# An early place for one expert's second weights, zero matmuls in one unit, and copies moved between engines, in a three-stage fp32 kernel

## The chip, the cores and the metric

The kernel runs on one core of a Trainium2 chip. The metric is the device time of one execution in microseconds (us). The kernel before was timed three times: 311.83, 313.52 and 314.58 us, median 313.52 us. One more execution was taken with the hardware profiler; its rows are what the prediction rests on.

## The reference

Three stages follow each other, all in fp32.

```python
# 1. attention-like recurrence: 4 batches x 8 heads, 768 tokens, head size 40
for t in range(S):
    m_new = maximum(f[t] + m, i[t])
    C = exp(f[t] + m - m_new) * C + exp(i[t] - m_new) * outer(v[t], k[t])
    n = exp(f[t] + m - m_new) * n + exp(i[t] - m_new) * k[t]
    y[t] = sigmoid(o[t]) * (C @ q[t]) / maximum(abs(n @ q[t]), 1)
# 2. soft mixture of 8 experts with 4 slots each, on the 3072 tokens x 320 features
logits = x @ phi
d = softmax(logits, over tokens)
slot_input = d.T @ x                      # 32 slots x 320
slot_out[e] = relu(slot_input[e] @ w1[e]) @ w2[e]     # 320 -> 1024 -> 320
x = softmax(logits, over slots) @ slot_out
# 3. feed-forward: 320 -> 1024 -> 320
h = x @ w_in
u = h * softmax(h)
out = ((u - mean(u)) / sqrt(var(u) + 1e-6) * g_ln) @ w_out
```

## The kernel before

The 3072 tokens are cut into 24 units of 128 (4 batches times 6 pieces of the sequence); `U[u]` holds what belongs to unit u. The program is one straight list of instructions for each engine, written out by hand: nothing is reordered later, so each engine works through its own list and waits where a buffer or an input is not ready.

**Stage 1, the units.** The loop at line 642 runs over the units. For unit i the strings in `ORDER` (line 32, taken in turn by i modulo 4) name the steps in the order in which they are issued, and `ops` (line 571) maps the names: `scA`, `scB` are the score products of unit i+1 (line 250), `R` the decay matrix of unit i+2 (lines 218, 219), `exp` its exponential on ScalarE (line 223), `wA`, `wB` the products of both on VectorE (line 254), `o0` to `o3` and `u0` to `u3` the outputs and state updates (lines 268, 271, 278), `sig0` to `sig2` the sigmoid of unit i+1 on ScalarE (lines 229, 231), `xT` the transpose of the finished unit i-2 (line 335). The inputs of a unit come in as `qk` (three buffers) and `kvo` (four buffers), issued two units ahead at the start of unit i (lines 138 to 144); tiles of the first expert weights, `w1s` (line 436), and raw 64-bit words of `w_in` and `w_out` (line 440) come in between. All transfers are issued by the SP queue, in order. They signal on eight semaphores in turn, so a transfer is issued only when the eighth before it has landed. Small transfers `gr` (line 196, 4 KB each) spread rows of the gates over partitions.

**Stage 2.** After the units come the softmax over tokens, `slot_input`, and the expert products: `w1_mm` (line 756) for both halves of the hidden layer, transposes (`hidden_T`), copies into `h2` (`hidden_ev`), then `w2_mm` (line 804). `w2_mm(0, ...)` uses the even experts 0, 2, 4, 6, four matmuls to a row block f; `w2_mm(1, ...)` the odd experts 1, 3, 5, 7. The eight tiles `w2s` (1280 KB each) stand where stage 1 had its buffers: the pool `p1` is closed at line 788 and the pool `tl` takes its space. Each load waits until the stage-1 tiles under it have been used for the last time. They are issued in the order 0, 2, 4, 6, 1, 3, 5, 7, and the last, expert 7, lies over `x_t`, which holds hidden values, and over `raw_t`, which holds the last tile of `w1`.

`wh` and `wl` (lines 815, 816) are the rounded upper part and the rest of `w_out`; `pe_cT` and `st_cT` (lines 428, 433) transpose the combine weights and copy them to `cT`; `sw` is `slot_out` times `w_in`.

**Stage 3.** For each unit: h (line 872), maximum, exponential, u, transposes (line 916), and three matmuls for each of the eight row blocks (lines 931 to 933), in the order of the strings `FIN_START` and `FIN`. It begins with the first h at about 190.6 us and is the same code before and after.

The places that the change touches in the code of before:

```python
    cT = cpool.tile([128, NU, 128], F32R, tag="cT", name="cT")         # line 77
    for e in order:                                                     # line 800
        SP.dma_start(out=w2s[e], in_=w2[e].rearrange("(c p) d -> p c d", p=128))
    w2_mm(0, range(1))                                                  # line 811
    hidden_ev(1, hidden_T(1))
    w2_mm(0, range(1, FC))
    w2_mm(1, range(FC))
    V.tensor_tensor(out=wl, in0=wo, in1=wh.bitcast(F32), op=ALU.subtract)
```

Of the kernel before, what the change touches and what calls it, by code (L numbers as in the profile page):

```python
# [7 lines left out]
F32 = mybir.dt.float32  # L8
F32R = mybir.dt.float32r
# [4 lines left out]
ALU = mybir.AluOpType  # L14
# [4 lines left out]
T = 128  # L19
NC = S // T  # L20
NU = NB * NC
NR = NH // 2
DV = D + 1
DM = NH * D
DF = 1024
NE, NS = 8, 32
FC = DF // 128
# [4 lines left out]
ORDER = (  # L32
# [4 lines left out]
)  # L37
HALVED = (0,)
# [6 lines left out]
def tile_kernel(  # L45
# [15 lines left out]
    V, A, G, PE, SP = nc.vector, nc.scalar, nc.gpsimd, nc.tensor, nc.sync  # L61

    cpool = ctx.enter_context(tc.tile_pool(name="cpool", bufs=1))
# [10 lines left out]
    hsel = cst[:, 432:440]  # L74
    bsel = cst[:, 440:444]
    phi_sb = cpool.tile([128, 3, NS], F32, tag="phi", name="phi_sb")
    cT = cpool.tile([128, NU, 128], F32R, tag="cT", name="cT")
    ones = cpool.tile([128, 128], F32, tag="ones", name="ones")
    one1 = cpool.tile([1, 1], F32, tag="one1", name="one1")
    acc = cpool.tile([128, DM + 1], F32, tag="acc", name="acc")  # L80
    sbd = cpool.tile([128, 20, 8], F32, tag="sbd", name="sbd")
    win = cpool.tile([128, 5, 512], F32, tag="win", name="win")
    wo = cpool.tile([128, FC, DM], F32, tag="wo", name="wo")
# [196 lines left out]
    def st_cd(u):  # L280
        c, b = divmod(u, NB)
        if c == 0 or c == NC - 1:
            return
        n = 64 + D
        U[u]["cd"] = cd_t
        EE("cd").tensor_tensor(out=U[u]["cd"][0:n], in0=C_t[b][0:n], in1=NAT[c][0:n, 64 + b * NR:64 + (b + 1) * NR].unsqueeze(2).to_broadcast([n, NR, 2 * DV]), op=ALU.mult)
# [141 lines left out]
            PE.transpose(ps[:, 128 * j:128 * j + 128], cs_t[g][:, j].rearrange("p q k s -> p (q k s)").bitcast(F32), ident)  # L428
        GR[g]["cTp"] = ps

    def st_cT(g):
        out, in_ = cT[:, 4 * g:4 * g + 4, :].rearrange("p j t -> p (j t)"), GR[g]["cTp"]
        A.copy(out=out, in_=in_)

    def load_w1(n):
        SP.dma_start(out=w1s[:, n, :], in_=w1p[n])

    def load_raw(n):
        raw = raw_t
# [41 lines left out]

    load_gates(0, T)
    V.memset(acc, 0.0)
    warm = ps_o.tile([128, 512], F32, tag="po", name="warm")

    def warm_up(n):
        for _ in range(n):
            PE.matmul(warm[:, 0:DM], acc[:, 0:128], acc[:, 0:DM], start=True, stop=True)

# [81 lines left out]
    def ops(i):  # L571
        c, b = divmod(i, NB)
        prv, nx1, nx2 = i >= 1, i + 1 < NU, i + 2 < NU
        T = {}
        for r in range(4):
            T[f"o{r}"] = lambda r=r: pe_out(i, r)
            T[f"u{r}"] = lambda r=r: pe_upd(i, r)
        T["cd"] = lambda: st_cd(i)
        if i >= 2:
            T["xT"] = lambda: pe_xT(i - 2)  # L580
            T["xTc"] = lambda: st_xT(i - 2)
        if prv:
            T["numa"] = lambda: st_num(i - 1, (0,))
            T["numb"] = lambda: st_num(i - 1, (1,))
            T["C"] = lambda: st_state(i - 1)
            for k in range(3):
                T[f"den{k}"] = lambda k=k: st_den(i - 1, k)
            T["sg"] = lambda: st_sg(i - 1)
            T["x"] = lambda: st_x(i - 1)
        if nx1:  # L590
            if i > 0:
                T["scA"] = lambda: pe_scores(i + 1, 0)
                T["scB"] = lambda: pe_scores(i + 1, 1)
            T["wA"] = lambda: st_w(i + 1, 0)
            T["wB"] = lambda: st_w(i + 1, 1)
            T["kw"] = lambda: st_kw(i + 1)
            for k in range(3):
                T[f"sig{k}"] = lambda k=k: st_sig(i + 1, (k,))
        else:
            T["scA"] = lambda: wo_mean(range(3))  # L600
        if nx2:
            T["R"] = lambda: pe_decay(i + 2)
            T["exp"] = lambda: st_exp(i + 2)
        dn = (i - 2) // 2 if 1 <= i < 22 else -1
        if dn >= 0:
            if i % 2 == 0:
                T["D0"] = lambda: decode(dn, 0)
            else:
                for n, k in (("D1", 1), ("D1b", 1.5), ("D2", 2), ("D3", 3), ("D4", 4)):
                    T[n] = lambda k=k: decode(dn, k)  # L610
        if i < 2:
            for k in range(1, 9):
                T[f"G{k}"] = lambda k=k: gate(128, S, k)
            for k in range(2):
                T[f"p{k}h"] = lambda k=k: gate_hi(128, S, k)
                T[f"p{k}l"] = lambda k=k: gate_lo(128, S, k)
        if i == 1:
            T["right"] = lambda: gate_right(1, range(NH))
        elif i > 1 and b and c + 2 < NC:
            js = [range(3 * b - 3, min(3 * b, NH)), range(4 * b - 8, 4 * b - 4)][i < NB]  # L620
            T["right"] = lambda: gate_right(c + 2, js)
        if i == 1 or b == 0 and 2 <= c + 1 < NC:
            T["left"] = lambda: gate_left(c + 1)
        ng = 1 if i == 2 else c + 1 if b == 0 and i else NC
        if ng < NC:
            T["gn"] = lambda: pe_gate(ng)
            T["gnc"] = lambda: gate_nat(ng)
        if i % 2 == 1 and i < 20:
            T["lraw"] = lambda: load_raw((i - 1) // 2)
        g = (i - 5) // 4  # L630
        if g >= 0:
            for k in range(3):
                T[f"tm{k}"] = lambda k=k: tok_max(g, k)
            T["lt"] = lambda: pe_logit(g)
            T["ltc"] = lambda: st_logit(g)
            T["nt"] = lambda: pe_natural(g)
            T["ntc"] = lambda: st_natural(g)
            T["sl"] = lambda: pe_slots(g)
            T["acc"] = lambda: st_acc(g)
        return T  # L640

    for i in range(NU):
        if 2 <= i < NU - 2:
            load_qk(i + 2)
            load_kvo(i + 2)
        if i == NU - 2:
            SP.dma_start(out=w1l, in_=w1p[19])
        T_ = ops(i)
        for t in ORDER[i % NB].split():
            if t in T_:  # L650
                T_[t]()
        if 3 <= i < 18:
            load_w1(i + 1)
        if i >= NU - 2:
            for f in range(FC // 2 * (i - NU + 2), FC // 2 * (i - NU + 3)):
                A.activation(out=wo[:, f, :], in_=wo[:, f, :], func=AF.Copy, scale=gl[:, f:f + 1])
# [131 lines left out]
    p1_ctx.close()  # L788
    w1_ctx.close()
    fin = ctx.enter_context(tc.tile_pool(name="fin", bufs=1, reuse_waits="tile"))  # L790

    tl_ctx = ExitStack()
    tl = tl_ctx.enter_context(tc.tile_pool(name="tl", bufs=1, side="right", reuse_waits="tile"))
    order = (0, 2, 4, 6, 1, 3, 5, 7)
    w2s = {7: tl.tile([128, FC, DM], F32, tag="w2s7", name="w2s7")}
    h2 = tl.tile([128, FC, 4, 2, 8], F32, tag="h2", name="h2")
    V.memset(h2, 0.0)
    for e in order[-2::-1]:
        w2s[e] = tl.tile([128, FC, DM], F32, tag=f"w2s{e}", name=f"w2s{e}")
    for e in order:  # L800
        SP.dma_start(out=w2s[e], in_=w2[e].rearrange("(c p) d -> p c d", p=128))
    wh = fin.tile([128, FC, DM], F32R, tag="wh", name="wh")
    wl = fin.tile([128, FC, DM], F32R, tag="wl", name="wl")
    def w2_mm(e2, fs):
        for f in fs:
            for m in range(4):
                PE.matmul(so_ps[32 * m:32 * m + 8, 0:DM], h2[:, f, m, e2, :], w2s[2 * m + e2][:, f, :], start=e2 == 0 and f == 0, stop=e2 == 1 and f == FC - 1)  # L807

    hidden_ev(0, hT0)
    V.tensor_tensor(out=wo, in0=wo, in1=wm.unsqueeze(1).to_broadcast([128, FC, DM]), op=ALU.subtract)  # L810
    w2_mm(0, range(1))
    hidden_ev(1, hidden_T(1))
    w2_mm(0, range(1, FC))
    w2_mm(1, range(FC))
    A.copy(out=wh, in_=wo)
    V.tensor_tensor(out=wl, in0=wo, in1=wh.bitcast(F32), op=ALU.subtract)
    scratch = fin.tile([128, DF], F32R, tag="u", name="scratch", bufs=3)
    one_hot = scratch[:, 0:768].rearrange("p (j k s) -> p j k s", j=4, k=3)
    eye4 = ident.rearrange("p (j s) -> p j s", j=4).unsqueeze(2).to_broadcast([128, 4, 2, NS])
# [26 lines left out]
    V.tensor_tensor(out=swl, in0=swc_ps, in1=swh.bitcast(F32), op=ALU.subtract)  # L846
    for k in range(2, 4):
        pe_cT(k)
    for k in range(2, 4):
        st_cT(k)  # L850
    sw = [fin.tile([128, 512], F32R, tag=f"swf{n}", name=f"swf{n}") for n in range(2)]
    for n in range(2):
        sw_ps = bank(("po", "pr")[n], f"sw_ps{n}")
        for j in range(2):
            for x, src in enumerate((swh, swl)):
                lhs = one_hot[:, 2 * n + j, 1 - x:3 - x].rearrange("p a s -> p (a s)")
                PE.matmul(sw_ps[:, 256 * j:256 * j + 256], lhs, src, start=x == 0, stop=x == 1)
        cp[n](sw[n], sw_ps)
    for k in range(4, NC):
        pe_cT(k)  # L860
        st_cT(k)
    tl_ctx.close()
    ps_ctx.close()

# [179 lines left out]
```

## Time and profile before

| | |
|---|---|
| median of three runs | 313.52 us (311.83 to 314.58) |
| the profiled execution, its own time | 316.18 us |
| span of the profile, first to last instruction | 314.4 us |
| TensorE (PE) busy | 296.1 us, 94% of the span |
| VectorE (DVE) busy | 244.6 us, 78% |
| ScalarE (ACT) busy | 217.1 us, 69% |
| GpSimd (POOL) busy | 72.1 us, 23% |
| transferred | 52.06 MB |
| first unit ends, last unit ends, first h of stage 3 | about 20, 153 and 190.6 us |

A busy PE is not PE at its peak: the profile counts an instruction as busy from its start to its modelled end. PEclk is the clock granted to TensorE, as a share of 2.4 GHz (1.00, or 0.50 for 1.2 GHz). PEld are the weight loads that go with the matmuls; in fp32 each matmul stands as two records. SPq is the queue that issues transfers. A note in square brackets gives the idle time of the engine just before the row and what ended it.

### The profile page before, as it was taken

The page shows a single profiled execution, that of the slowest core. Times are in us where ns is not written, and L with a number is a line of the kernel's source. Part 1 is how long each engine was busy: PE and PEld are TensorE (multiplying, and loading weights), DVE is VectorE, ACT ScalarE, POOL GpSimd, SP SyncE. Part 2 cuts the span into 40 slices and gives each one's busy share as a digit, 9 for nine tenths or more (in the row PEclk, how much of TensorE's full clock was granted, in tenths as well). Part 3 has the DMA queues.
Part 4 walks back from the last instruction along what each step waited for, and adds up shares of the span by engine and source line. Part 5 has one row for each costly group of instructions (what it writes and reads, how often), then busy time and mean ns, then how long its engine had stood idle before and what let it go on. Part 6 is the DMA issues. An engine that isn't in the chain of part 4 may idle for free.

```text
span 314.4 us, 8424 instructions
## 1 busy us (share of the span) xinstructions
PE 296.1 (94%) x3333; PEld 236.4 (75%) x3333; DVE 244.6 (78%) x526; ACT 217.1 (69%) x469; POOL 72.1 (23%) x105
## 2 busy tenths in 40 slices
PE   7985999988999999989999797999999999999995
PEld 4564787765787777767642345999999999999995
DVE  8688589876899999999658417998888787787851
ACT  5375576647667757858624527798898888988983
POOL 5412064454355465364102200000000000000000
PEclk9997599997999999999999999999999999999999
DMA  6976788888999998778998500011011011010111
GB/s 166 277 174 260 222 269 286 238 294 240 285 281 292 292 305 286 240 229 272 364 361 302 170 2 0 0 46 42 24 41 44 21 44 43 21 44 25 41 42 42
DMA packets 26086, 52.06 MB, mean 166 GB/s; under 512 B 3904, under 2 KB 15872, under 8 KB 26048
## 3 DMA queue, kind: packets, MB, share of 16 engines
q1 hardware_dynamic: 26048, 51.53, 51.4%
q8 instruction: 26, 0.43, 0.6%
q14 instruction: 12, 0.10, 0.1%
HBM read 47.03 MB, written 3.93 MB: 162 GB/s over the span
## 4 chain that ended last, share of the span: by engine, by line
PE 74%; DVE 10%; DMA 8%; ACT 3%; issue 2%; POOL 1%; SPq 1%; POOLq 0%; ACTq 0%; DVEq 0%
PE o L933 9%; PE o L931 9%; PE o L932 9%; PE uT L916 7%; PE sc L250 7%; PE po L268 5%; DMA kvo<-kvo 4%; PE h L872 3%; PE R L218 3%; PE xTp L335 3%; PE R L219 3%; DMA w2s<-w 2%; PE pr L271 2%; DVE lb L254 2%; PE so_ph L807 1%
## 5 line engine op out<-in xcount | busy, mean ns | idle before, releaser
L931 PE MATMUL o<-wh,uh 128*128 128x320 f32 x192 | 62.9, 327 | 0.0
L933 PE MATMUL o<-wh,ul 128*128 128x320 f32 x192 | 59.2, 308 | 0.0
L932 PE MATMUL o<-wl,uh 128*128 128x320 f32 x192 | 58.9, 307 | 0.0
L891 DVE SCALAR_TENSOR_TENSOR u<-h,e 128x1024 f32<-128x1024 f32 (+1 forms) x25 | 29.4, 1181 | 16.4 <-ACT e L884 16.4
L268 PE MATMUL po<-kvo,lb 128*64 128x41 f32 x768 | 38.4, 232 | 0.8 <-PE sc L250 0.8
L250 PE MATMUL sc<-qk 64*128 64x128 f32 x384 | 35.7, 308 | 2.1 <-DMA qk<-qkp 1.8
L254 DVE TENSOR_TENSOR lb<-sc,lb 128x512 f32<-128x512 f32 x48 | 31.3, 676 | 7.6 <-PE sc L250 4.8
L932 PEld LDWEIGHTS o<-wl,uh 128*128 128x128 f32 x192 | 36.2, 188 | 0.9
L931 PEld LDWEIGHTS o<-wh,uh 128*128 128x128 f32 x192 | 36.1, 188 | 0.9
L250 PEld LDWEIGHTS sc<-qk 64*128 64x128 f32 x384 | 28.8, 205 | 10.5 <-issue 3.8
L268 PEld LDWEIGHTS po<-kvo,lb 128*64 128x64 f32 x768 | 31.1, 141 | 6.7 <-issue 3.2
L933 PEld LDWEIGHTS o<-wh,ul 128*128 128x128 f32 x192 | 36.0, 187 | 0.0
L924 DVE TENSOR_TENSOR ul<-uT,uh 128x512 fp32r<-128x512 f32 x48 | 33.0, 688 | 3.3 <-ACT uh L920 3.3
L920 ACT CAST uh<-uT 128x512 fp32r<-128x512 f32 x48 | 28.1, 585 | 9.4 <-PE uT L916 8.7
L231 ACT ACTIVATE kvo<-kvo 128x320 f32<-128x320 f32 x48 | 22.6, 472 | 16.7 <-DMA kvo<-kvo 16.2
L916 PE MATMUL uT<-cst,u 128*128 128x128 f32 x192 | 28.8, 273 | 1.6 <-DVE u L891 1.6
L877 DVE TENSOR_REDUCE st<-h 128x1 f32<-128x1024 f32 x24 | 29.2, 1215 | 1.4 <-PE h L872 1.4
L884 ACT ACTIVATE e<-h,st 128x1024 f32<-128x1024 f32 (+1 forms) x25 | 26.7, 1069 | 3.5 <-DVE st L877 3.3
L903 ACT ACTIVATE e<-u,st 128x1024 f32<-128x1024 f32 x24 | 27.7, 1154 | 1.9 <-DVE st L897 1.9
L223 ACT ACTIVATE lb<-R 128x1024 f32<-128x1024 f32 x24 | 24.3, 1012 | 5.8 <-PE R L219 5.7
L218 PE MATMUL R<-gr,gl 128*128 128x512 f32 x48 | 26.3, 607 | 0.0
L916 PEld LDWEIGHTS uT<-cst,u 128*128 128x128 f32 x192 | 23.8, 141 | 2.2 <-DVE u L891 2.0
(241 smaller groups left out, 587.4 us busy)
## 6 DMA issues: line engine op xcount, KB each, us to landing
kvo<-kvo SPq DMA_DIRECT2D x24, 484.0 KB
w2s<-w SPq DMA_DIRECT2D x8, 1280.0 KB
w1s<-w1p SPq DMA_DIRECT2D x19, 512.0 KB
raw<-w SPq DMA_DIRECT2D x10, 512.0 KB
qk<-qkp SPq DMA_DIRECT2D x24, 160.0 KB
qk<-qkp SPq DMA_DIRECT2D x48, 80.0 KB
out<-ob SPq DMA_DIRECT2D x24, 160.0 KB
gt<-gates SPq DMA_DIRECT2D x1, 640.0 KB
```

Of the source, the lines that this page charges most:

```text
L218: PE.matmul(U[u]["R"][:, a], gl_t[c % 2][:, b, :], gr_t[c % 2][:, a * NR:(a + 1) * NR, :], start=True, stop=False)
L250: PE.matmul(U[u]["sc", a][:, r, :], t[p, 0, r, :], t[p, 1, r, :], start=True, stop=True)
L254: V.tensor_tensor(out=lb[:, a * NR:(a + 1) * NR, :], in0=U[u]["sc", a], in1=lb[:, a * NR:(a + 1) * NR, :], op=ALU.mult)
L268: PE.matmul(U[u]["po"][t, 2 * r + a, :], U[u]["lb"][:, a * NR + r, t], va(u, 2 * r + a), start=True, stop=True)
L877: V.tensor_reduce(out=F[i]["st"][:, 0:1], in_=F[i]["h"], axis=AX.XY, op=ALU.max, negate=True)
L891: V.scalar_tensor_tensor(out=F[i]["u"][:, c], in0=F[i]["h"].rearrange("p n f -> p (n f)")[:, c], scalar=1.0, in1=F[i]["e"][:, c], op0=ALU. ...
L916: PE.transpose(ps[:, k, :], F[i]["u"][:, (4 * n + k) * 128:(4 * n + k + 1) * 128], ident)
L920: A.copy(out=F[i]["uh"][:, 4 * n:4 * n + 4, :], in_=F[i]["uT", n])
L924: V.tensor_tensor(out=F[i]["ul"][:, c, :], in0=F[i]["uT", n], in1=F[i]["uh"][:, c, :].bitcast(F32), op=ALU.subtract)
L931: PE.matmul(o, uh, wh[:, k, :], start=k == 0, stop=False)
L932: PE.matmul(o, uh, wl[:, k, :], start=False, stop=False)
L933: PE.matmul(o, ul, wh[:, k, :], start=False, stop=k == FC - 1)
```

## The change

Five edits. (1) `w2s0`, expert 0 of the second weights, has its own tile, and is loaded at the end of unit 1; the other seven stay in the `tl` pool. (2) `cT` leaves the first pool, to make room for it, and stands in the last pool, `fin`. (3) `wl` is computed by GpSimd instead of VectorE; three instead of one row blocks of `w2_mm(0, ...)` stand ahead of the transposes of the second half. (4) Two of the six copies to `cT` go to VectorE, and one of ScalarE's comes after its copy of `sw`. (5) Six matmuls on a tile of zeros (128 x 320 each) stand in unit 2 ahead of `xT`; their result isn't used.

```diff
- "numa D1b xT tm1 scA numb D1 C scB den0 xTc tm2 D2 nt ntc sig0 den1 R o0 den2 o1 gn gnc sl sg sig1 u3 kw o3 wA wB cd o2 x exp acc u1 u2 u0 D0 sig2 right",
+ "numa D1b W xT tm1 scA numb D1 C scB den0 xTc tm2 D2 nt ntc sig0 den1 R o0 den2 o1 gn gnc sl sg sig1 u3 kw o3 wA wB cd o2 x exp acc u1 u2 u0 D0 sig2 right",
...
-    cT = cpool.tile([128, NU, 128], F32R, tag="cT", name="cT")
+    w2s0 = cpool.tile([128, FC, DM], F32, tag="w2s0", name="w2s0")
...
-    def st_cT(g):
+    def st_cT(g, eng=1):
         out, in_ = cT[:, 4 * g:4 * g + 4, :].rearrange("p j t -> p (j t)"), GR[g]["cTp"]
-        A.copy(out=out, in_=in_)
+        cp[eng](out, in_)
...
+    w2s = {0: w2s0}
+
+    def load_w2(e):
+        SP.dma_start(out=w2s[e], in_=w2[e].rearrange("(c p) d -> p c d", p=128))
...
-    warm = ps_o.tile([128, 512], F32, tag="po", name="warm")
-
-    def warm_up(n):
+    def warm_up(n, tag="po"):
+        warm = ps_o.tile([128, 512], F32, tag=tag, name=f"warm_{tag}{n}")
         for _ in range(n):
             PE.matmul(warm[:, 0:DM], acc[:, 0:128], acc[:, 0:DM], start=True, stop=True)
...
+        if i == 2:
+            T["W"] = lambda: warm_up(6, "misc")
...
+        if i == 1:
+            load_w2(0)
...
+    cT = fin.tile([128, NU, 128], F32R, tag="cT", name="cT")
...
-    w2s = {7: tl.tile([128, FC, DM], F32, tag="w2s7", name="w2s7")}
...
-    for e in order[-2::-1]:
+    for e in order[:0:-1]:
         w2s[e] = tl.tile([128, FC, DM], F32, tag=f"w2s{e}", name=f"w2s{e}")
-    for e in order:
-        SP.dma_start(out=w2s[e], in_=w2[e].rearrange("(c p) d -> p c d", p=128))
+    for e in order[1:]:
+        load_w2(e)
...
-    w2_mm(0, range(1))
+    w2_mm(0, range(3))
     hidden_ev(1, hidden_T(1))
-    w2_mm(0, range(1, FC))
+    w2_mm(0, range(3, FC))
...
-    V.tensor_tensor(out=wl, in0=wo, in1=wh.bitcast(F32), op=ALU.subtract)
+    G.tensor_tensor(out=wl, in0=wo, in1=wh.bitcast(F32), op=ALU.subtract)
...
-    for k in range(2, 4):
-        st_cT(k)
+    st_cT(2, 0)
...
         cp[n](sw[n], sw_ps)
+    st_cT(3)
     for k in range(4, NC):
         pe_cT(k)
-        st_cT(k)
+        st_cT(k, k % 2)
```

The SP queue at the end of unit 1 and in units 2 and 3, before (`raw` are the raw words, `qk_0_123` and `kvo_116` the inputs of unit 4, `qk_0_121` and `kvo_115` those of unit 5):

```order
L440 DMA raw_94<-w 128x1024
L138 DMA qk_0_123<-qkp 40x1024
L140 DMA qk_0_123<-qkp 40x512 x2
L144 DMA kvo_116<-kvo 128x968
L196 DMA gr_77<-m_130 8x128 x4
L138 DMA qk_0_121<-qkp 40x1024
L140 DMA qk_0_121<-qkp 40x512 x2
L144 DMA kvo_115<-kvo 128x968
```

The same place after:

```order
L445 DMA raw_94<-w 128x1024
L441 DMA w2s_63<-w 128x8x320
L138 DMA qk_0_123<-qkp 40x1024
L140 DMA qk_0_123<-qkp 40x512 x2
L144 DMA kvo_116<-kvo 128x968
L196 DMA gr_77<-m_130 8x128 x4
L138 DMA qk_0_121<-qkp 40x1024
L140 DMA qk_0_121<-qkp 40x512 x2
L144 DMA kvo_115<-kvo 128x968
```

The transfer of expert 0 (`w2s_63`) now stands ahead of the inputs of unit 4, and one of the four small `gr` transfers behind them is the eighth after it.

The SP queue at the end of stage 1, before (`raw` here is the last tile of `w1`; the number after `w2s` is the expert):

```order
L647 DMA raw0_94<-w1p 128x1024
L801 DMA w2s0_2422<-w2 128x8x320
L801 DMA w2s2_2421<-w2 128x8x320
L801 DMA w2s4_2420<-w2 128x8x320
L801 DMA w2s6_2419<-w2 128x8x320
L801 DMA w2s1_2418<-w2 128x8x320
L801 DMA w2s3_2417<-w2 128x8x320
L801 DMA w2s5_2416<-w2 128x8x320
L801 DMA w2s7_2413<-w2 128x8x320
```

The same place after:

```order
L653 DMA raw0_94<-w1p 128x1024
L441 DMA w2s2_2431<-w2 128x8x320
L441 DMA w2s4_2430<-w2 128x8x320
L441 DMA w2s6_2429<-w2 128x8x320
L441 DMA w2s1_2428<-w2 128x8x320
L441 DMA w2s3_2427<-w2 128x8x320
L441 DMA w2s5_2426<-w2 128x8x320
L441 DMA w2s7_2425<-w2 128x8x320
```

Seven loads are left, and each expert takes the place in memory, and with it the wait, that the one ahead of it in the list had: expert 2 that of expert 0, and so on, expert 7 that of expert 5. The place of expert 7, over `x_t` and `raw_t`, is left free.

TensorE at the start of unit 2, before (`dps` ends unit 1, `xTp` is the transpose of unit 0, `sc` the scores of unit 3):

```order
L278 MATMUL dps<-kvo_115 40x41 x4
L335 MATMUL xTp_398<-cst,x_92 128x128 x3
L250 MATMUL sc_0_402<-qk_0_125 128x128
L250 MATMUL sc_1_403<-qk_0_125 128x128
L250 MATMUL sc_0_402<-qk_0_125 128x128
```

The same place after:

```order
L278 MATMUL dps<-kvo_115 40x41 x4
L492 MATMUL warm_misc_400<-acc 128x320 x6
L335 MATMUL xTp_407<-cst,x_92 128x128 x3
L250 MATMUL sc_0_411<-qk_0_125 128x128
L250 MATMUL sc_1_412<-qk_0_125 128x128
```

The six matmuls on zeros stand between the last update of unit 1 and the transpose of unit 0.

## Rows read from the trace of the kernel before

**Rows 1.** The page's slices: granted TensorE clock, in tenths, 40 slices.

```profile
PEclk9997599997999999999999999999999999999999
```

**Rows 2.** Chain of waits, 172 to 191 us: start, us, what.

```profile
172.45 7.42 DMA w2s<-w
...
188.99 1.07 ACT cT L433 x2
190.06 0.54 ACT swf L729
```

**Rows 3.** Timeline of the weight loads, 172 to 180 us: start, us, instruction, idle before.

```profile
172.94 0.20 PEld L766 LDWEIGHTS hT<-cst,acc 128*128 128x128 f32 x2 [0.67 <-ACT acc L754]
...
177.45 0.10 PEld L807 LDWEIGHTS so_ph<-w2s,h 128*8 128x8 f32 x3 [0.17 <-issue]
179.91 0.12 PEld L807 LDWEIGHTS so_ph<-w2s,h 128*8 128x8 f32 x8 [2.36 <-DMA w2s<-w]
```

**Rows 4.** SP queue, 160 to 173 us: what it waited for (us, times, longest).

```profile
SPq L801 <- PE ph L761: 2.6, 1, 2.6
```

**Rows 5.** SP queue, timeline, 161 to 163 us: the seventh load of `w2s`.

```profile
161.80 1.69 SPq L801 DMA_DIRECT2D w2s<-w  x1
```

**Rows 6.** Windows: PE, PEld, DVE, ACT, POOL busy, then granted clock, DMA share, GB/s.

```profile
26.00:28.00 2.00, 0.00 (x0) 0.00 (x0) 1.97 (x5) 1.48 (x5) 0.73 (x1) 0.92 1.01 410
32.00:34.00 2.00, 2.00 (x19) 1.08 (x17) 0.42 (x1) 0.00 (x0) 0.00 (x0) 0.50 0.91 294
34.00:36.00 2.00, 2.00 (x34) 1.93 (x32) 0.76 (x2) 1.11 (x3) 0.00 (x0) 0.50 0.83 286
36.00:38.00 2.00, 2.00 (x19) 1.44 (x14) 1.50 (x3) 1.98 (x4) 0.00 (x0) 0.52 0.61 201
38.00:40.00 2.00, 2.00 (x35) 1.49 (x33) 1.37 (x6) 1.78 (x4) 0.94 (x1) 1.00 0.46 68
...
72.00:74.00 2.00, 1.92 (x6) 1.18 (x6) 1.25 (x4) 1.97 (x4) 0.00 (x0) 0.52 0.85 312
...
168.00:170.00 2.00, 2.00 (x21) 0.48 (x14) 1.72 (x5) 0.52 (x2) 0.00 (x0) 1.00 1.07 362
```

**Rows 7.** Timeline of PE at 28 and 41 us.

```profile
28.13 0.90 PE L335 MATMUL xTp<-cst,x 128*128 128x128 f32 x3 [3.15 <-POOL x L330]
...
40.95 0.50 PE L218 MATMUL R<-gr,gl 128*128 128x512 f32 x1
```

**Rows 8.** Timeline of the SP queue, 30 to 39 us.

```profile
30.38 0.45 SPq L440 DMA_DIRECT2D raw<-w  x1
...
32.11 0.35 SPq L144 DMA_DIRECT2D kvo<-kvo  x1
...
38.18 0.35 SPq L144 DMA_DIRECT2D kvo<-kvo  x1
```

**Rows 9.** SP queue, 36 to 40 us: what it waited for.

```profile
SPq L144 <- DMA kvo<-kvo: 1.9, 1, 1.9
```

**Rows 10.** Timeline of ACT, 38 to 41 us.

```profile
38.19 0.47 ACT L231 ACTIVATE kvo<-kvo 128x320 f32<-128x320 f32 x1 [0.21 <-DMA kvo<-kvo]
...
39.07 1.01 ACT L223 ACTIVATE lb<-R 128x1024 f32<-128x1024 f32 x1
```

**Rows 11.** Timeline of PE at 150 us: six records of 128 x 320 matmuls.

```profile
149.90 1.78 PE L478 MATMUL warm<-wo,bsc 128*128 128x320 f32 x6
```

**Rows 12.** Timelines of POOL at 39 us, of DVE from 176 us, of PE at 197 us.

```profile
39.05 1.27 POOL L463 TENSOR_TENSOR win<-win,dsc 128x512 f32<-128x512 f32 x1 [7.92 <-DVE win L459]
...
176.64 2.83 DVE L816 TENSOR_TENSOR wl<-wo,wh 128x2560 fp32r<-128x2560 f32 x1 [2.63 <-ACT wh L815]
184.43 0.49 DVE L823 COPY so_sb<-so_ph 128x320 f32<-128x320 f32 x1 [4.96 <-PE so_ph L807]
...
197.42 0.31 PE L932 MATMUL o<-wl,uh 128*128 128x320 f32 x1
```

**Rows 13.** Chain of waits, 60 to 69 us.

```profile
62.04 6.52 DMA kvo<-kvo
```

## The prediction

> **What bounds the kernel now.** I read the page's slices first, then the chain of waits, then the timeline of the stretches that the change touches, and last the SP queue, since two of the five edits move transfers. The slices [rows 1] show a TensorE that holds its full clock, 2.4 GHz, in nearly every slice; the dents are one in slices 4 and 5 (31 to 39 us, units 2 and 3) and one around 72 us. TensorE is the engine that the chain mostly runs over, so what an edit is worth is the time by which TensorE's list moves, in stage 1 and at the change to stage 3 apart.
>
> Three places matter. First, the end of stage 2: the chain sits for 7.42 us on the last load of second expert weights [rows 2]. It was issued only at 172.45 us, because the queue first waited 2.6 us for a matmul of L761 [rows 4]. Not all of it is lost: TensorE worked through what it had, and its weight loads stood idle for 2.36 us, from the group at 177.45 us until 179.91 us [rows 3]. Between groups in this loop 0.16 to 0.17 us is usual, so the lost time is 2.36 - 0.16 = 2.2 us.
>
> Second, unit 2: TensorE has nothing to do for 3.15 us, until GpSimd has written x at about 28.1 us [rows 7]. The granted clock falls during that idle time: the window from 26 to 28 us has 0.92, so the drop came 2 x 0.08 / 0.5 = 0.3 us before its end. It is 0.50, which is 1.2 GHz, until shortly before 38 us (36 to 38 us still 0.52) [rows 6]. That is some 10.2 us at half clock.
>
> Third, the transfers of units 2 and 3. The inputs `kvo` of unit 4 are issued at 32.11 us and are what ScalarE waits for at 38.19 us; the SP queue itself waits 1.9 us for the same transfer before it issues the next `kvo` at 38.18 us [rows 8 to 10]. So `kvo` of unit 4 landed at 38.1 us, and behind it on ScalarE stands the exponential of unit 5 (39.07 us, ending at 40.08), which frees the bank that TensorE's next decay matrix needs: that one starts at 40.95 us [rows 7, 10]. The slack of this path against TensorE is only 40.95 - 40.08 = 0.87 us.
>
> **The change part by part.** The sum is made against the profiled execution, 316.18 us; the median of the runs is 2.66 us lower, and I carry the difference over to it.
>
> (a) *Seven loads at the end instead of eight.* Each expert takes the place, and so the wait, of the one ahead of it in the list. Expert 7 gets that of expert 5, whose load was issued at 161.80 us [rows 5] instead of 172.45 us. The transfers stand queued from there: 362 GB/s at 168 to 170 us with a DMA share of 1.07 [rows 6], so one load of 1.31 MB takes 1.31 / 362 = 3.6 us; the load that was issued at 161.80 us in this trace was used at 177.45 us without a wait [rows 3]. The 2.2 us are gone, and I find nothing else late behind them: the experts of the even half are each in earlier than before. What comes next is TensorE's own list.
>
> (b) *Three row blocks ahead of the second transposes.* The weight loads stood idle for 0.67 us before L766 at 172.94 us, waiting for ScalarE [rows 3]. Against the 0.16 us that are usual, 0.2 to 0.5 us of it can be filled with matmuls that have to run anyway. I take 0.2, since part of the idle time is the start of a transpose on any order. (a) and (b) together: -2.4 us, bounds -1.8 (a little of the wait turns up again on the copies into `h2`) and -2.8.
>
> (c) *`wl` on GpSimd.* VectorE took 2.83 us for it [rows 12]. GpSimd takes 1.27 us for 512 columns of two inputs, so five times that, 6.35 us, for 2560. It starts when `wh` is done, 176.64 us in this trace and half a microsecond later behind (b), and ends about 183.5 us; the first matmul that needs it is L932 at 197.42 us [rows 12]. More than 10 us of cover; 0. VectorE gains nothing, since its next work, the copy at 184.43 us, waited 4.96 us for TensorE anyway [rows 12].
>
> (d) *Copies to `cT`.* On the chain, ScalarE's two copies at 188.99 us are followed by its copy of `sw` at 190.06 us [rows 2]. Taken out of the way, the copy of `sw` still needs its matmuls, which end at about the same time. Gain at most the 0.3 us of one short wait, loss at most 0.2 us if the copy on VectorE holds up its own half of `sw`; I take 0.
>
> (e) *Six zero matmuls.* They are 12 records, and six records of this shape take 1.78 us at full clock [rows 11], so 12 take 3.6 us at most. The gap is 3.15 us [rows 7], which nobody else uses. Cost 0 to 0.4 us where the clock is full. What they can give: TensorE keeps 2.4 GHz through units 2 and 3, where it would have been through earlier by several us. But it can't pass the decay matrix at 40.95 us by more than the slack of the path over `kvo` of unit 4, 0.87 us. So their worth is between -0.87 us and +0.4 us, if the transfers stay where they are.
>
> (f) *The early load.* They don't stay. The queue issues it between the raw words (30.38 us) and the inputs of unit 4, so those have 1.31 MB more ahead of them: 3.6 us at 362 GB/s. If it fills only idle transfer time, the delay is 0: the windows from 32 to 38 us have shares of 0.91, 0.83 and 0.61 [rows 6], which is 2 x (0.09 + 0.17 + 0.39) = 1.3 us unused. If none of that is filled, `kvo` of unit 4 lands at 38.1 + 3.6 = 41.7 us, ScalarE's exponential ends 1.9 us after that, as before, and the decay matrix starts at 43.6 instead of 40.95 us: +2.7 us. If all of it is filled, +1.4 us. The queue is also held up itself: the eighth transfer behind the load may go only when the load has landed, which delays the inputs of unit 5 as much. I take +2.0, the middle of these two, since the transfers stood close to saturated there, and the zero matmuls then give nothing: TensorE would only wait earlier. I see no slack further on that would give it back: by 62 us a `kvo` is on the chain again, for 6.52 us [rows 13], and it is issued in step with TensorE.
>
> That the transfers pass one another little is also what the Trainium skill says ("DMA: Bandwidth & Descriptors", queues, rings and completion order): on each DMA engine the descriptors are consumed in ring order. By that rule alone the load's whole 3.6 us would come before the inputs of unit 4, and (f) would be +2.7 and the time 313.8 us. The row at 38.19 us agrees in that `kvo` came in late behind `qk`, but doesn't show how much idle time a longer queue would fill.
>
> The sum: -2.4 (a, b) + 0 (c, d) + 2.0 (e, f) = -0.4 us: 315.8 us for an execution like the profiled one, 313.1 us beside the median. A difference under 1% (3.1 us) can hardly be told from no change here.
>
> **The rivals.** *The load is hidden.* The idle transfer time around it, and a queue in which small inputs pass the large load, let `kvo` of unit 4 land as before. For it: the DMA share at 38 to 40 us is only 0.46 [rows 6]. Against it: that idle time comes after the transfer that is waited for. Then (f) is 0, (e) gives up to 0.87, and the time is 313.5 - 2.4 - 0.9 = 310.2 us, or 311.1 without (e).
>
> *The clock falls one unit later (slower).* TensorE, quick through unit 2, runs out of work in unit 3 because `qk` of unit 4 stands behind the load, and is granted half clock again. For it: this is what followed the idle 3.15 us in unit 2, and again at 72 us, where 72 to 74 us has 0.52 [rows 6], after the wait for `kvo` in the units around it. Against it: some waits pass without a drop. The price: the stretch in units 2 and 3 lasted 10.2 us, half of which, 5.1, is the loss if all of it stands on the path; the short one at 72 us cost at least 2 x 0.48 = 1 us. Between them, some 3.5 us, as part of it lies beside the wait for the load: 313.1 + 3.5 = 316.6 us. It decides from an idle stretch in unit 3 of about the 3.15 us seen in unit 2. The Trainium skill ("TensorE: Matmul & The Clock Gate", HAM oscillation) describes the same: a wait for a transfer throttles TensorE, and the work after it starts at half rate.
>
> *The wait at the end stays.* Another load is last there, for instance because the seven start later, and (a) gives nothing: 313.5 + 2.0 = 315.5 us. Against it: the place that waited for L761 is not used any more.
>
> **How the numbers follow.** The forecast 0.45, load hidden 0.29, clock one unit later 0.20, wait at the end stays 0.06. The likeliest is 313.1 us; its own range is 311.3 (f at +0.6) to 314.5 (f at +2.7, a and b at -1.8). The whole range takes in the hidden case (310.2), less the 0.4 us by which (a, b) can be better, 309.8, rounded out a little, and reaches to a little over the slower rival: 309.6 to 317.0 us. Faster by over 1% (under 310.4 us) holds two thirds of the hidden case and a little of the forecast's lower side: 0.24. Slower by over 1% (over 316.7 us) holds half of the slower rival and a little of the rest: 0.16. Within 1%: 0.60.
>
> **What would show it.** Right: in the profile after, no idle time on `w2s` in TensorE's loop over the second weights; the ScalarE wait for `kvo` of unit 4 at 41 us instead of 38.2, and the decay matrix of unit 6 at about 43 us instead of 40.95; GpSimd's `wl` over long before stage 3. Wrong: that decay matrix at 40 us or earlier (the load hidden), or a granted clock of 0.50 in units 3 and 4 with everything from 45 us on shifted by 4 us or more, or TensorE idle on w2s at the end of stage 2 as before.

## The result: 1.2% slower

The changed kernel took 317.48 us, the median of 20 runs (314.62 to 321.24), and the kernel before 314.36 us, the median of 20 beside it: a ratio of 1.012, 95% interval 1.008 to 1.016, or +3.1 us by the medians. The profiled execution took 318.71 us with a span of 316.9 us, 2.5 us over that of before. The ratios leave out runs more than 1.5% above the fastest of their kernel, and single runs of this kernel scatter by some 2 us, so the table further down gives the difference of the medians beside each ratio (of e14's twelve runs only four stand in its ratio).

The granted clock after, in 40 slices, to be held against [rows 1]. Before, the dent stands in slices 4 and 5, 24 to 39 us. After, a small one is left in slice 6 (40 to 48 us), and deeper ones stand in slice 2 (8 to 16 us) and in slice 16 (119 to 127 us):

```profile
PEclk9599989998999997999999999999999999999999
```

The dent in slice 2 lies ahead of all that the change touches, and costs nothing by unit 2: the transpose of unit 0 starts at 28.10 us, and at 28.13 before. Such dents move between executions of one kernel: in a second trace of the changed kernel (e14) they lie at 24 to 27 and 37 to 47 us. A reading from one pair of traces is therefore weak, and where more traces bear on it they are named.

The chain that ended last, split by engine, of the kernel before and then of the changed one. Transfers went from 8 to 21% of the span, but that doesn't single out the load: a trace without it (e4) has 25%, and e14 has 17%.

```profile
PE 74%; DVE 10%; DMA 8%; ACT 3%; issue 2%; POOL 1%; SPq 1%; POOLq 0%; ACTq 0%; DVEq 0%
```
```profile
PE 64%; DMA 21%; DVE 6%; ACT 3%; issue 2%; POOL 2%; SPq 1%; POOLq 0%; ACTq 0%; DVEq 0%
```

**Units 2 and 3.** Timeline of the SP queue after, 30 to 42 us (answers to [rows 8]), and below it the queue's own waits there:

```profile
30.72 0.43 SPq L441 DMA_DIRECT2D w2s<-w  x1
...
32.62 0.35 SPq L144 DMA_DIRECT2D kvo<-kvo  x1
33.07 6.81 SPq L196 DMA_DIRECT2D gr<-m  x4
39.98 0.40 SPq L138 DMA_DIRECT2D qk<-qkp  x1
...
41.25 0.36 SPq L144 DMA_DIRECT2D kvo<-kvo  x1
```
```profile
SPq L196 <- DMA w2s<-w: 4.4, 1, 4.4
```

`kvo` of unit 4 goes out about as early as before (32.62 us against 32.11), but behind the load. The next four small transfers stand 4.4 us for the load to land, and everything that follows in the list with them: `kvo` of unit 5 goes out at 41.25 us instead of 38.18.

PE and then ACT after, in the same stretch (to [rows 7, 10]):

```profile
33.97 0.55 PE L335 MATMUL xTp<-cst,x 128*128 128x128 f32 x3
...
38.24 0.46 PE L250 MATMUL sc<-qk 64*128 64x128 f32 x2 [2.31 <-DMA qk<-qkp]
39.37 2.04 PE L250 MATMUL sc<-qk 64*128 64x128 f32 x14 [0.66 <-DMA qk<-qkp]
...
43.34 0.49 PE L218 MATMUL R<-gr,gl 128*128 128x512 f32 x1
```
```profile
40.53 0.47 ACT L231 ACTIVATE kvo<-kvo 128x320 f32<-128x320 f32 x1 [4.27 <-DMA kvo<-kvo]
41.41 1.01 ACT L223 ACTIVATE lb<-R 128x1024 f32<-128x1024 f32 x1
...
45.75 0.47 ACT L231 ACTIVATE kvo<-kvo 128x320 f32<-128x320 f32 x1 [2.60 <-DMA kvo<-kvo]
```

Before, `xT` of unit 1 stood here:

```profile
36.34 0.90 PE L335 MATMUL xTp<-cst,x 128*128 128x128 f32 x3
```

TensorE came through unit 2 at full clock, began `xT` of unit 1 2.4 us sooner than before, and then stood 2.31 + 0.66 = 2.97 us for `qk` of unit 4. The windows (columns as in [rows 6]) show what follows:

```profile
38.00:40.00 2.00, 1.09 (x8) 0.96 (x10) 0.00 (x0) 0.00 (x0) 0.60 (x1) 0.84 0.69 200
40.00:42.00 2.00, 2.00 (x26) 1.78 (x26) 0.95 (x2) 1.44 (x3) 0.00 (x0) 0.50 0.34 121
42.00:44.00 2.00, 2.00 (x43) 1.68 (x39) 1.22 (x4) 1.16 (x3) 1.72 (x3) 0.80 0.80 189
```

The granted clock goes to 1.2 GHz one unit later than before, for 0.6 + 2.0 + 0.8 = 3.4 us. This is no chance of one trace. All six traces that have the load at the end of unit 1 in one piece (this one, e1, e3, e9, e14, e15) show both: ScalarE waits 2.7 to 4.5 us for `kvo` of unit 4, and TensorE has 1.2 GHz at 42 us, in a stretch of 3.4 to 10.2 us. In the twelve others that wait is at most 1.1 us, and the clock is full from 41 to 48 us.

**The end of stage 2.** PE, DVE, ACT and POOL after (to [rows 2, 3, 12]):

```profile
174.16 0.66 PE L774 MATMUL hT<-cst,x 128*128 128x128 f32 x4
176.46 1.80 PE L815 MATMUL so_ph<-w2s,h 128*8 128x320 f32 x24
...
178.78 7.18 PE L815 MATMUL so_ph<-w2s,h 128*8 128x320 f32 x104
...
192.75 0.73 PE L880 MATMUL h<-swf,cT 128*128 128x512 f32 x2 [0.29 <-ACT cT L737]
```
```profile
186.03 0.49 DVE L831 COPY so_sb<-so_ph 128x320 f32<-128x320 f32 x1 [6.92 <-PE so_ph L815]
```
```profile
191.63 0.59 ACT L737 CAST swf<-sw_ps 128x512 fp32r<-128x512 f32 x1 [1.65 <-PE sw_ps L864]
192.11 1.08 ACT L737 CAST cT<-cTp 128x512 fp32r<-128x512 f32 x2
```
```profile
181.71 5.64 POOL L824 TENSOR_TENSOR wl<-wo,wh 128x2560 fp32r<-128x2560 f32 x1 [1.67 <-issue]
```

The wait for `w2s` is gone: the 104 records run in one piece. From the first transposes to the first h it takes 192.75 - 174.16 = 18.59 us; before it was 190.61 - 169.86 = 20.75:

```profile
169.86 0.66 PE L766 MATMUL hT<-cst,x 128*128 128x128 f32 x4
...
190.61 0.71 PE L872 MATMUL h<-swf,cT 128*128 128x512 f32 x2
```

So this part (the tail from here on) is 2.16 us shorter, all ahead of it 4.3 us longer, and stage 3 0.4 us longer.

### The profile page after: what moved, and what is told of

It reads as the page before. It is cut to its first block, busy times and chain, and to the rows that moved or that the text cites. A ratio compares the mean times of both kernels' runs of the same rounds, so it can differ in the third digit from the quotient of the medians.

```text
span 316.9 us, 8449 instructions
## 1 busy us (share of the span) xinstructions
PE 295.8 (93%) x3345; PEld 236.8 (75%) x3345; DVE 244.7 (77%) x527; ACT 216.1 (68%) x467; POOL 78.7 (25%) x106
## 4 chain that ended last, share of the span: by engine, by line
PE 64%; DMA 21%; DVE 6%; ACT 3%; issue 2%; POOL 2%; SPq 1%; POOLq 0%; ACTq 0%; DVEq 0%
DMA kvo<-kvo 13%; PE o L939 9%; PE o L940 9%; PE o L941 9%; PE uT L924 7%; DMA qk<-qkp 6%; PE sc L250 4%; PE h L880 4%; PE po L268 4%; PE so_ph L815 3%; DMA w1s<-w1p 2%; PE pr L271 2%; PE xTp L335 2%; PE so_ph L769 1%; PE ph L769 1%
## 5 line engine op out<-in xcount | busy, mean ns | idle before, releaser
L250 PE MATMUL sc<-qk 64*128 64x128 f32 x384 | 34.1, 301 | 5.6 <-DMA qk<-qkp 4.5
L250 PEld LDWEIGHTS sc<-qk 64*128 64x128 f32 x384 | 27.7, 199 | 13.0 <-issue 5.4
L928 ACT CAST uh<-uT 128x512 fp32r<-128x512 f32 x48 | 28.1, 585 | 10.2 <-PE uT L924 9.5
L218 PE MATMUL R<-gr,gl 128*128 128x512 f32 x48 | 24.9, 575 | 3.5 <-ACT lb L223 1.2
```

The lines of the kernel that those rows point to most:

```text
L250: PE.matmul(U[u]["sc", a][:, r, :], t[p, 0, r, :], t[p, 1, r, :], start=True, stop=True)
L928: A.copy(out=F[i]["uh"][:, 4 * n:4 * n + 4, :], in_=F[i]["uT", n])
```

## The experiments

Theory L: the early load is the loss. Theory Z: the zero matmuls and the clock in unit 3 are. Theory T: the tail's edits are. All ratios and differences are to the kernel before, run beside each on the same chip. e1 to e4 shared one chip, and so did e5 to e8, e9 to e12 and e13 to e16. There are 12 runs each, but 7 of e3 and 6 of e7, e11 and e16; with single runs that scatter by 2 us, a difference of medians is good to about 0.8 us (an estimate).

| run | median, us | difference | ratio, 95% interval |
|---|---|---|---|
| e1 no zero matmuls | 317.63 | +3.14 | 1.004 (1.000 to 1.008) |
| e2 load late | 313.12 | -1.37 | 0.994 (0.991 to 0.997) |
| e3 before + load | 317.48 | +2.99 | 1.009 (1.005 to 1.013) |
| e4 before + zero matmuls | 313.52 | -0.97 | 0.996 (0.993 to 0.999) |
| e5 late, no zero matmuls | 315.82 | -0.05 | 0.998 (0.993 to 1.002) |
| e6 late, old copies | 313.24 | -2.63 | 0.990 (0.985 to 0.994) |
| e7 load at unit 10 | 319.29 | +3.42 | 1.011 (1.005 to 1.017) |
| e8 eight pieces | 316.16 | +0.28 | 1.003 (0.999 to 1.007) |
| e9 w1 two units later | 319.04 | +4.00 | 1.010 (1.006 to 1.015) |
| e10 before + w1 later | 314.37 | -0.67 | 0.989 (0.984 to 0.993) |
| e11 as e6 + w1 later | 311.89 | -3.15 | 0.985 (0.979 to 0.992) |
| e12 as e6, `wl` on VectorE | 313.32 | -1.72 | 0.993 (0.988 to 0.997) |
| e13 no load | 313.48 | -2.36 | 0.992 (0.988 to 0.996) |
| e14 changed kernel again | 318.94 | +3.10 | 1.000 (0.993 to 1.007) |
| e15 before + load + zero matmuls | 318.86 | +3.02 | 1.012 (1.008 to 1.016) |
| e16 as e11 again | 313.50 | -2.34 | 0.989 (0.983 to 0.996) |

**Parts undone, parts alone (e1 to e4).**

```diff
- "numa D1b W xT tm1 ...          # e1, from the changed kernel
+ "numa D1b xT tm1 ...
-        if i == 1:               # e2
-            load_w2(0)
+        if 18 <= i < 22:
+            load_w2(0, range(2 * i - 36, 2 * i - 34))
+        if i == 1:               # e3, from the kernel before
+            SP.dma_start(out=w1s[...], in_=w2[0]...)
- "numa D1b xT tm1 ...            # e4, from the kernel before
+ "numa D1b W xT tm1 ...
```

> The changed kernel without the six zero matmuls. Theory L (the early load alone costs, by holding back the inputs of units 4 and 5): nothing changes, 1.012 +- 0.003 of the kernel before; transposed rows of unit 0 start near 34 us again and PE waits for qk as before. Theory Z (the zero matmuls and the clock that falls in unit 3 carry the loss): the time falls by 1 to 2 us, ratio 1.006 or less. The clock row of 38 to 44 us tells which.

> The changed kernel with the early load of expert 0's w2 moved to units 18 to 21, in four pieces of 320 KB behind the units' own instructions, after the last w1 load of stage 1. Theory L: stage 1 ends as before the change and the tail keeps its gain of 2.7 us less 0.5 for the late copies: 0.993 of the kernel before (0.990 to 0.998). Theory Z: the loss stays but for the tail, 0.998 to 1.004. Theory T (the tail's edits bring nothing net, and stage 1's loss is a chance of the trace): 1.00.

> The kernel before with one extra load of expert 0's w2 (1.28 MB) at the end of unit 1, into the places of three w1 tiles that are loaded much later; its data is not used, and all eight loads at the end stay. Theory L: it loses all that the load costs, with no gain at the end: +4 to +5.5 us, 1.013 to 1.018. The prediction's term was +2.0 (1.006). Theory Z: under 1.006.

> The kernel before with the six zero matmuls in unit 2 and nothing else of the change. Theory L: 1.000 +- 0.003, the matmuls lie in time in which PE waits. Theory Z: 1.003 or more, with the clock low in unit 3. A third outcome, a gain up to 0.9 us (0.997), would come from unit 2's transposes starting earlier at full clock.

The load alone loses 3.0 us by the medians, and moved to where the w1 loads are over, the changed kernel beats the kernel before. That is theory L, though its +4 to +5.5 us for e3 was too much. The zero matmuls alone gain 1.0 us (the third outcome of e4), in an interval that ends just below 1. With the load they are worth nothing by the medians: e1 and the changed kernel have the same difference. By its ratio (1.004 against 1.012) e1 lies where theory Z put it. The clock row that was to decide speaks against Z: without zero matmuls too, e1 falls to 1.2 GHz between 38 and 44 us.

```profile
38.00:42.00 4.00, 3.81 (x63) 3.54 (x63) 1.89 (x4) 2.59 (x5) 2.43 (x4) 0.67 0.47 134
42.00:46.00 4.00, 4.00 (x55) 2.79 (x56) 1.95 (x7) 0.44 (x2) 0.60 (x1) 0.91 0.87 276
```

Where the zero matmuls gain shows in e4's timelines of ACT and PE: the `kvo` of unit 4 is there at 37.13 us and the decay matrix of unit 6 at 39.06, 1.9 us sooner than in [rows 7] (not all of it by the zero matmuls, see (e) below).

```profile
37.13 0.47 ACT L231 ACTIVATE kvo<-kvo 128x320 f32<-128x320 f32 x1 [0.55 <-DMA kvo<-kvo]
```
```profile
39.06 0.50 PE L218 MATMUL R<-gr,gl 128*128 128x512 f32 x1 [0.36 <-ACT lb L223]
```

**The tail, and where the load may stand (e5 to e8).**

```diff
- "numa D1b W xT tm1 ...          # e5, from e2
+ "numa D1b xT tm1 ...
-    st_cT(2, 0)                  # e6, from e2
+    for k in range(2, 4):
+        st_cT(k)
...
-    st_cT(3)
...
-        st_cT(k, k % 2)
+        st_cT(k)
-        if i == 1:               # e7, from the changed kernel
+        if i == 10:
             load_w2(0)
-            load_w2(0)           # e8, from the changed kernel
+        if 1 <= i < 9:
+            load_w2(0, range(i - 1, i))
```

> The late load of e2 (four pieces in units 18 to 21) without the six zero matmuls: the tail's edits alone, with nothing of the change left ahead of unit 18. Theory L: 0.994 of the kernel before, as e2 within 0.003. If the zero matmuls bring the gain that they showed alone (0.996): 0.998. If they cost: 0.990.

> The late load of e2 with the zero matmuls, and with the copies of the combine weights as before (all on ScalarE, each right behind its transposes). If the moved copies cost the 0.5 us that the trace after the change suggests (first h late behind two ScalarE copies): 0.992, and the first h starts 0.5 us sooner after hT of chunk 0 than in e2. If they are worth what they bring later (the remaining copies shared with VectorE): 0.994 or above.

> The changed kernel with the one load of 1.28 MB at the end of unit 10 instead of unit 1, where every unit moves kvo, qk and a w1 tile. Theory L1 (the load costs where the transfers are the limit, and that is so all through units 3 to 17): a loss of +2 to +3 in stage 1 less the tail's 2.2: 1.000 (0.997 to 1.004). Theory L2 (only the first units, where few kvo are ahead, can't take it): 0.994, as with the late load. Theory Z: 1.00 or above.

> The changed kernel with the early load cut in eight pieces of 160 KB, one at the end of each of units 1 to 8. Theory of the block (1.28 MB in one piece stands ahead of unit 4's and 5's inputs in the queue): most of the loss goes, 0.994 to 1.000, and the kvo of unit 4 lands by 39 us. Theory of the bytes (that stretch has no room for 1.28 MB, however cut): 1.003 to 1.010.

e5 against e2 gives the zero matmuls 1.3 us, but across two chips and within the scatter. e5 itself, the tail's edits with the load late, isn't told from the kernel before (0.998), though the tail is 2.16 us shorter in the trace. Part of the reason may lie in the moved copies. e6, PE at the end of stage 2:

```profile
167.47 0.66 PE L775 MATMUL hT<-cst,x 128*128 128x128 f32 x4
...
185.54 0.71 PE L881 MATMUL h<-swf,cT 128*128 128x512 f32 x2
```

That is 18.07 us against 18.59: with the old copies the first h doesn't stand behind ScalarE's two late ones. The same two values come back in every trace: 18.58 to 18.60 us in the nine with the moved copies (this kernel, e1, e2, e5, e7, e8, e9, e13, e14), 18.05 to 18.07 in the four that have the tail's other edits without them (e6, e11, e12, e16).

The moved copies do more. TensorE's wait for the first u of stage 3 is 2.15 to 2.17 us in the nine, and 1.58 to 1.61 us in the nine other traces. Before, and then after:

```profile
194.85 1.27 PE L916 MATMUL uT<-cst,u 128*128 128x128 f32 x8 [1.59 <-DVE u L891]
```
```profile
197.02 1.27 PE L924 MATMUL uT<-cst,u 128*128 128x128 f32 x8 [2.15 <-DVE u L899]
```

In five of the nine (e1, e5, e7, e8, e9), and in no other trace, the granted clock falls to 1.2 GHz within 2 us behind this wait, for 3.4 us. From the first transposes to the end of the program it takes 142.3 us with the old copies, 142.7 to 142.9 us with the moved ones where the clock stays, and 144.0 to 144.2 us where it falls; with the whole tail of before (before, e3, e4, e10, e15) it is 143.7 to 144.7 us. So the moved copies cost 0.5 us in every trace and some 1.3 us more in about half of them. e6's median agrees (-2.63 against -1.37), within the scatter.

At unit 10 the load costs as much as at unit 1, so L2 falls; L1's 1.000 was too low as well. e7's PE and ACT, then e4's, which has no load there:

```profile
88.65 0.46 PE L250 MATMUL sc<-qk 64*128 64x128 f32 x2 [2.92 <-DMA qk<-qkp]
...
90.99 0.90 PE L335 MATMUL xTp<-cst,x 128*128 128x128 f32 x3
```
```profile
90.88 0.47 ACT L231 ACTIVATE kvo<-kvo 128x320 f32<-128x320 f32 x1 [6.25 <-DMA kvo<-kvo]
```
```profile
86.27 0.46 PE L250 MATMUL sc<-qk 64*128 64x128 f32 x2 [0.46 <-DMA qk<-qkp]
...
88.19 0.55 PE L335 MATMUL xTp<-cst,x 128*128 128x128 f32 x3
```

At 74 and 80 us the two traces are within 0.1 us of each other. The load is issued at 78.6 us; in the unit behind it e7 is 2.8 us late, one unit later 5.6 us, and its granted clock is 1.2 GHz for 10.2 us from 89 us on. So waits and a fallen clock behind the block are nothing special to units 2 and 3.

Cut in eight pieces (e8) the load costs 0.28 + 2.36 = 2.6 us over e13, which has none: half of what the one block does. Its ratio, 1.003, is where the theory of the bytes begins; `kvo` of unit 4 came by 39 us, as the theory of the block had it. In e8 the queue isn't held up (the same four `gr` take 2.42 us instead of 6.81), and no wait for `kvo` of unit 4 is left, though ScalarE takes it up as late as 38.60 us: the clock fell in unit 2, in spite of the zero matmuls. `kvo` of unit 5 is waited for there, 3.09 us against 2.17 in e4.

```profile
34.07 2.42 SPq L196 DMA_DIRECT2D gr<-m  x4
```
```profile
38.60 0.47 ACT L231 ACTIVATE kvo<-kvo 128x320 f32<-128x320 f32 x1
```

**Bytes or place (e9 to e12).**

```diff
-        if 3 <= i < 18:          # e9 from the changed kernel, e10 from before, e11 from e6
-            load_w1(i + 1)
+        if 5 <= i < 20:
+            load_w1(i - 1)
-    G.tensor_tensor(out=wl,      # e12, from e6
+    V.tensor_tensor(out=wl,
```

> The changed kernel (early load at unit 1, zero matmuls, its own copies) with the fifteen w1 loads of units 3 to 17 moved two units later, to units 5 to 19: after unit 4 the queue has moved 1.28 MB more and 1.05 MB less, and nothing else differs. Theory of the bytes (units 3 to 17 are limited by what the queue must move, and any 1.28 MB more ahead of unit 18 costs its landing time): most of the loss goes, 0.993 to 1.000. Theory of the place (the block ahead of unit 4's kvo costs its 2 to 3 us there, and the rest of the loss is chance): 1.003 to 1.010.

> The kernel before with the fifteen w1 loads two units later and nothing of the change. Theory of the bytes: stage 1 ends 2 to 4 us sooner, 0.988 to 0.994, if the loads that move to units 18 and 19 find room there. Theory of the place: 1.000 +- 0.003.

> The version of e6 (late load, zero matmuls, old copies) with the w1 loads two units later as well. Theory of the bytes: faster than e6 (0.990) by what e10 gains, less what 1.28 MB beside two w1 tiles cost in units 18 and 19: 0.982 to 0.990. Theory of the place: 0.990.

> The version of e6 with the low half of wo taken on VectorE again, as before the change. The prediction has it at nothing: 0.990 +- 0.004, and from the transposes of chunk 0's hidden rows to the first h it takes 18.07 us, as in e6, because VectorE only waits for the second projection there. If VectorE's copies stand on the chain, the stretch grows by up to 2.8 us, to 0.998.

e9 moves 1.05 MB out of the way from unit 3 on, and loses as much as before. Its `kvo` of unit 4 is 4.41 us late for ScalarE. Against e10, which has the same w1 loads and no early load, its decay matrix of unit 6 is 4.4 us late, and that of the last unit still is:

```profile
41.68 0.47 ACT L231 ACTIVATE kvo<-kvo 128x320 f32<-128x320 f32 x1 [4.41 <-DMA kvo<-kvo]
```

So bytes taken out of the queue behind the block don't make up for it: the place counts, ahead of inputs that are needed within the time that the block takes to land. That bytes cost something as well isn't excluded, since e8 still loses half. The whole load straight behind the inputs of unit 4, which would part the two, was not run. e10 is inconclusive: its ratio says 0.989 and its median -0.67 us. e12 agrees with (c): on either engine `wl` is no part of the chain, and the stretch to the first h is 18.05 us (171.80 to 189.85 us) on VectorE.

**What the parts add up to (e13 to e16).**

```diff
-        if i == 1:               # e13, from the changed kernel
-            load_w2(0)
...
+    G.memset(w2s0, 0.0)
     L, g = NU - 1, NC - 1
# e14: the changed kernel   # e15: e3 and e4 together   # e16: e11
```

> The changed kernel without any load of expert 0's w2 (its place is set to zero on GpSimd behind stage 1, so the second projection of that expert is left out of the result): tail edits and zero matmuls, no early load. If the load costs 5 us inside the changed kernel: 0.990 to 0.994 of the kernel before, 4.5 to 6 us under e14. If it costs 3 and the tail's gain is not all kept: 0.997 to 1.002.

> The changed kernel again, beside e13 and e15 on one chip: 1.012 +- 0.004 of the kernel before.

> The kernel before with the six zero matmuls and with one extra load of expert 0's w2 at the end of unit 1, as in e3, its data not used; the tail is that of the kernel before. If the wait for the inputs behind the load swallows the zero matmuls' gain: as e3 or 1 us more, 1.009 to 1.013, and 1.8 to 2.1 us over e14 if the tail's gain is kept. If the zero matmuls keep their gain beside the load: 1.005.

> The version with the w2 load late, the w1 loads two units later, the zero matmuls and the copies as before, again: 0.985 +- 0.006 of the kernel before; if the first measurement was lucky, 0.990, as without the moved w1 loads.

e13, timelines of SP, ACT and PE, to be held against the changed kernel's above:

```profile
31.90 2.42 SPq L196 DMA_DIRECT2D gr<-m  x4
```
```profile
36.35 0.47 ACT L231 ACTIVATE kvo<-kvo 128x320 f32<-128x320 f32 x1 [0.61 <-DMA kvo<-kvo]
```
```profile
38.28 0.50 PE L218 MATMUL R<-gr,gl 128*128 128x512 f32 x1 [0.41 <-ACT lb L223]
```

Without the load the decay matrix of unit 6 starts at 38.28 us, with it at 43.34: 5.1 us, and the spans differ by 316.9 - 311.7 = 5.2. e14, the same kernel run beside e13, has the decay matrix at 43.74 us, 5.5 us late, but a span of 314.6 us, only 2.9 us longer: there nearly half of the delay was given back along stage 1. The medians of e14 and e13 say 318.94 - 313.48 = 5.5 us, their ratios 2.6 us (1.000, where 1.012 was expected, and 0.992). So inside the changed kernel the load costs between 2.6 and 5.5 us. Where it stood beside the zero matmuls it also swallowed what they had gained.

The parts don't close fully. Tail and zero matmuls are worth 2.4 us (e13), the zero matmuls alone 1.0 (e4), so the tail 1.4. By the traces the tail is worth about 1.5 us, or 0.2 us where the clock falls in stage 3. Load and zero matmuls together cost 3.0 (e15), level with e14 and not 1.8 to 2.1 us above it. Less the tail that would be +1.6 to +2.8, and +3.1 was measured twice. What of the rest, 0.3 to 1.5 us, is more than scatter stays open.

## Why the prediction was wrong

**(a, b)** Right. No wait for `w2s` is left; without the moved copies the first h comes 2.7 us sooner after the transposes (20.75 to 18.07), and the end of the program about 2.0 us (144.3, the mean of five traces, to 142.3). -2.4 was foretold.

**(c)** Right: 5.64 us on GpSimd (6.35 estimated), over at 187.35, 5.4 us ahead of the first h.

**(d)** A second miss, of size. Put at 0 with at most 0.2 us lost; 0.5 was measured in every trace (18.59 against 18.07), and 1.3 more in the five of nine where the clock fell in stage 3. The prediction looked at what stood ahead of the copy of `sw`, and not at what the first h needs: the ScalarE copies now come behind it.

**(e)** Wrong in its bound. It said that the decay matrix can't come more than 0.87 us sooner, because `kvo` of unit 4 lands at 38.1 us. It took that landing for fixed. In e4 and e13 it lands at 37.1 and 36.3 us, and the decay matrix starts 1.9 and 2.7 us sooner than before. About 1 us of this is the trace of before and not the zero matmuls: there `kvo` of unit 4 took 6.1 us from its issue to landing, and 4.95 us in e5 and e10, whose instructions up to there are the same, without zero matmuls. Nor is the gain sure: in e2 and e12 the clock fell between 33 and 40 us in spite of the zero matmuls, and the decay matrix came at 41.8 and 41.7 us. In time e4 puts it at 1.0 us, where the load isn't in the way.

**(f)** This is the step that failed: the term +2.0 for (e) and (f) together was too small. Its first half was right: the ScalarE wait for `kvo` of unit 4 went to 40.53 us ("41"), the decay matrix to 43.34 ("about 43"). But +2.0 was the delay against one trace of the kernel before, whose unit 2 ran at half clock, and it was entered with a gain of 0 for (e). Against the same kernel without the load that decay matrix is 5.1 to 5.5 us late (after and e14 against e13, e15 against e4), and 0.7 and 2.8 us where neither kernel has the zero matmuls (e1 and e3 against before). The gain of (e) was there and was lost. In time the load measured +3.0 us alone (e3), +4.0 us beside the zero matmuls (e15 less e4) and +2.6 to +5.5 us inside the changed kernel. The upper bound of +2.7 took 3.6 us for the transfer less the path's slack of 0.87 us; it had no term for the clock, which fell again in all six traces with the load at unit 1.

The prediction also saw "no slack further on that would give it back". The runs show both. Against the trace of before, this kernel's decay matrices are 2.4 us late at unit 6, about 1.0 us at units 12 to 15, behind the dent that before has at 72 us, and 4.1 to 4.3 us from unit 20 on. Against e13, e14 goes from 5.5 to 2.9 us, and the changed kernel's first trace from 5.1 over 3.8 to 5.5.

The rival "the clock falls one unit later" describes most of what happened, and its 316.6 us was the nearest to 317.48: TensorE quick through unit 2, idle for 2.97 us in unit 3, and 3.4 us at 1.2 GHz after it. It was given 0.20 because it stood against the forecast as an alternative. The two were one event: the same late transfers stand ahead of both in all six traces. By the ring-order rule of the Trainium skill ("DMA: Bandwidth & Descriptors", queues, rings and completion order) (f) would have been +2.7; the trace agrees only in part: `kvo` (40.53 us) came behind the load, for which the queue waited until 39.3 us, but the first `qk` behind the load let TensorE go on at 38.24 us, and the same sentence of the Trainium skill lets a later write finish first. e3's +3.0 lies nearer to +2.7 than +2.0 did.

The version that beats both kernels leaves expert 0's load to units 18 to 21 in four pieces and the copies as they were: e6, 0.990. With the w1 loads two units later as well it was 0.985 and 0.989 (e11, e16), which is not told apart from e6.

## What to carry to other kernels

A large load put ahead of inputs that are needed soon held the work up here by 0.7 to 2.8 us where the units were slow anyway and by 5.1 to 5.5 us where they were not, for a transfer of 3.6 us (1.31 MB at 362 GB/s). Against the same kernel without the load, 2.6 to 5.5 us were left at the end. Free transfer time on average says nothing of it: look for a stretch in which nothing is waited for, or cut the load in pieces, which saved half of it in e8. Where one edit speeds a stage up and another delays its inputs, price the delay against the kernel with the first edit, not against the kernel before.

## What had not been expected

One load of 1.28 MB cost as much in unit 10 as in unit 1 (+3.4 and +3.1 us with the tail's gain in both). And two copies moved from ScalarE to VectorE lengthened a wait by 0.6 us, and in five traces of nine the clock fell there; why in these five and not in the others, no run shows.
